# Logit products of a linear-attention, cosine-FFN and soft-MoE kernel gathered from four groups a block into two, with a longer ring of activation tiles

## The chip, the cores and the metric

The kernel runs on one core of one Trainium2 chip. The metric is device time in microseconds (us) of one execution. TensorE (PE) multiplies matrices into PSUM; VectorE (DVE) and ScalarE (ACT) do the elementwise work; GpSimd (POOL) does little here; SyncE (SP) issues the DMAs. Each engine takes its own instructions in program order, so an instruction that waits holds up all that stand behind it on that engine.

## What is computed

```python
# attention: 8 batches, 8 heads, 576 tokens, head size 64
kv  = einsum('bhsd,bhse->bhde', k, v)
out = einsum('bhsd,bhde->bhse', q, kv)
x   = out / sqrt(mean(out*out, -1) + 1e-6) * g_norm     # 4608 tokens x 512
# feed-forward: 512 -> 2048 -> 512
h = x @ w_in
g = h * cos(h)
x = g @ w_out
# soft mixture of experts: 8 experts x 4 slots = 32 slots
logits = x @ phi
d = softmax over tokens(logits);  slot_input = d.T @ x
slot_out[e] = relu(slot_input[e] @ w1[e]) @ w2[e]
return softmax over slots(logits) @ slot_out
```

## The kernel before

The 4608 tokens are cut into `NB` = 12 blocks j of `TB` = 384 tokens, and the 2048 columns of h into `NF` = 16 tiles f of 128. A step is one (j, f). The order of the work on every engine is written out by hand: at each step the program runs what is registered in `loads` (DMAs), then `main`, then `side` (other TensorE work and what goes with it), `cos_a`, `post`, `cos_b`, `cos_c`, `fin`. `at2(j, f, ...)` registers an entry in `side`; an f of 16 or more belongs to the next block, so "step 18 of block j" is step 2 of block j+1. Blocks 0 and 1 are interleaved; blocks 2 to 11 run one after the other. Block 11 and the expert layers behind it (`tail`) are ordered differently.

`main` (L378) computes one tile of h: twelve products of 128x128 by 128x384 into one of three PSUM banks of the pool `ps_m`. The cosine is a chain between ACT and DVE: `fr` (L396) and `tt` (L398) on ACT, the rounding (L403) on DVE, the sine (L408) on ACT, and the product g = h cos h (L443) on DVE, which is the last reader of the bank. So the product `main` of tile f+3 needs the L443 of tile f. The result lies in a slot of `ring`, 128x384 each. In blocks 2 to 10 DVE then transposes it into `tr` (L449), from where `regroup` DMAs bring it to `g`.

`w_out` and `phi` are folded into `wp`, so the logits of a block are 16 products of 128x32 by 128x384, one a tile, in `logits` (L491): four neighbours write the four quarters of the partitions of one bank. In blocks 2 to 10 there were four calls, `c` = 0 to 3, at steps 6, 10, 14 and 18 (`4 * c + PLAN["lg"]`), each taking four tiles out of the ring. `l_evac` (L510) copies the bank at step 18, `l_add` (L516) sums the quarters at step 19, then `l_max`, `l_exp`, `l_T` (L561, step 22) and `slot_acc` (L585, step 26, "ab") follow for the running softmax over tokens.

The attention of block j+1 is computed inside block j: `att_out` (L203) at steps 4, 8 and 11, `att_xs` (L224) one step later, `att_xT` (L235 on TensorE, then L239 on ACT) at steps 7, 11 and 14, `att_lo` (L248 on DVE). `kv_pair` (L184, L187) computes k'v for two heads, followed by two copies into `kvA` (L140, on DVE); four of them make a batch. For batches 4 to 7 they stand in blocks 4, 5, 7 and 8, two at step 14 and two at step 18. They, `att_out`, `att_xT`, `l_add`, `l_T` and `slot_acc` share the four PSUM banks `ps_a`.

`ring_next` hands out the first free slot of the ring: seven slots, and three more in blocks 0 and 1. `load_q` brings q for block j into one of two buffers, `q0` and `q1`, at step 13 of block j-2. Late in the kernel, `fill` loads the experts' weights, in a fixed order of pieces of 256 KB, into buffers that are free by then, `q0` at step 13 of block 9 and `q1` at step 12 of block 10 among them; `tail` refills them in the order of the lists `early` and `mid`.

Of the kernel before, what the change touches and what calls it, by code (L numbers as in the profile page):

```python
# [8 lines left out]
F32 = mybir.dt.float32  # L9
# [12 lines left out]
PLAN = dict(  # L22
    ke=(0, 0),
    lp=(0, 0, 0),
    wE=0,
    gE=(0, 0),
    nt=(1, (12, 16, 20, 24), (1, 2), (2, 1), (3, 1), 4),
    rx=0,
    nq=(0, 0),
    nl=3,  # L30
# [10 lines left out]
    stop=None,  # L41
    start=(
# [4 lines left out]
    ),  # L47
# [3 lines left out]
    pm=3,  # L51
    pa=4,
    lag=0,
    lg=6,
    le=18,
    la=19,
    lx=(3, 1),
# [6 lines left out]
    xs=(1, 1, 1),  # L64
    xT=(7, 11, 14),
    lo=(1, 0, 0),
    kv=(14, 14, 18, 18),
    rg=(11, 18),
    kvl=0,
    ql=13,  # L70
# [4 lines left out]
def tile_linear_attention__ffn_cos__soft_moe(  # L75
# [19 lines left out]
    NB = qT.shape[0]  # L95
    TB = qT.shape[2] * qT.shape[4]

    SP = 2
    const = ctx.enter_context(tc.tile_pool(name="const", bufs=1))
    w_p = ctx.enter_context(tc.tile_pool(name="w", bufs=1))  # L100
    x_p = ctx.enter_context(tc.tile_pool(name="x", bufs=1))
    g_p = ctx.enter_context(tc.tile_pool(name="g", bufs=1))
    t_p = ctx.enter_context(tc.tile_pool(name="t", bufs=1))
    gt_p = ctx.enter_context(tc.tile_pool(name="gt", bufs=1))
    dr_p = ctx.enter_context(tc.tile_pool(name="dr", bufs=1, space=bass.MemoryType.DRAM))
    tmp_p = ctx.enter_context(tc.tile_pool(name="tmp", bufs=2))
    kv_p = ctx.enter_context(tc.tile_pool(name="kvp", bufs=4))
    rem_p = ctx.enter_context(tc.tile_pool(name="rem", bufs=1))
    q_p = ctx.enter_context(tc.tile_pool(name="qp", bufs=1))
# [23 lines left out]
    ring = [[None, gT_all[:, i, :], 0] for i in range(7)]  # L133
# [16 lines left out]
        return [(0, 128, 2 * p + (i if i < 2 else t // 2))]  # L150

    def load_q(j):
        t = q_p.tile([128, 3, 4, 128], F32, tag=f"q{j % 2}", name="q")
        if j == 0:
            for t3 in range(3):
                nc.sync.dma_start(out=t[:, t3], in_=qT[j][:, t3])
        else:
            nc.sync.dma_start(out=t, in_=qT[j])
        q_t[j] = t
# [204 lines left out]
    h_t, gT_t, g_t, tr_t = {}, {}, {}, {}  # L364

    def on_pe(j, f):
        return j < 2 or j == NB - 1
# [63 lines left out]
        run(fin, j, f)  # L431

    def ring_next(j, f):
        i = next(i for i, r in enumerate(ring) if (r[0] not in gT_t or j == NB - 1)
                 and (not r[2] or j == 0 or j == 1 and f < 10))
        _, g, extra = ring.pop(i)
        ring.append([(j, f), g, extra])
        return g

    def cos_c(j, f):  # L440
        fr = fr_t.pop((j, f))
        g = ring_next(j, f)
        nc.vector.tensor_tensor(out=g, in0=fr, in1=h_t.pop((j, f)), op=ALU.mult)  # L443
        gT_t[j, f] = g
        if not on_pe(j, f):
            h, o = divmod(f, 8)
            if o == 0:
                tr_t[j, h] = t_p.tile([128, 12, 8, 32], F32, tag=("TA", "TB")[h], name="tr")
            nc.vector.transpose(out=tr_t[j, h][:, :, o, :], in_=g.rearrange("p (b t) -> p b t", t=32))  # L449
# [36 lines left out]
    def logits(j, c):  # L486
        if c == 0:
            l_t[j] = ps_l.tile([128, TB], F32, tag="l", name="l")
        for o in range(4):
            f = 4 * c + o  # L490
            nc.tensor.matmul(out=l_t[j][32 * o:32 * o + 32, :], lhsT=wp[:, f, :], rhs=gT_t.pop((j, f)),  # L491
                             start=(c == 0), stop=(c == (2 if j == NB - 1 else 3)))

    def logits2(j, f):
        if (j, f) == (0, 0):
# [329 lines left out]
    def at(j, f, fn, *a):  # L825
        side.setdefault((j, f), []).append((fn, a))
# [8 lines left out]
    def U(j, f):  # L835
        if j == 0 and f >= NF:
            j, f = 1, f - L
        return j + f // NF, f % NF

    def at2(j, f, *a):  # L840
        at(*U(j, f), *a)
# [6 lines left out]
    def end(j, f, fn, *a):  # L848
        fin.setdefault((j, f), []).append((fn, a))
# [6 lines left out]
    def ld_at(j, f, fn, *a):  # L856
        loads.setdefault(U(j, f), []).append((fn, a))

    for j in range(NB):
        for f in range(NF):  # L860
            if on_pe(j, f):
                at2(j, f + (1 if j == 1 and f < NF // 2 else 2), gtr, j, f)
        for h in range(2):
            if (j, h) == (NB - 2, 1):
                for x in range(4):
                    ld_at(NB - 1, x + PLAN["lag"], regroup, j, h, (x,))
            elif not on_pe(j, 8 * h):
                for x in range(4):
                    ld_at(j, PLAN["rg"][h] + x * PLAN["rx"], regroup, j, h, (x,))
        if j == 0:  # L870
            for f in range(NF):
                at2(0, f + PLAN["wT"], wp_kk, f)
                at2(0, f + PLAN["wM"], wp_sum, f)
        if j < 2:
            for f in range(0, NF, 2):
                late_in = j and f + 3 + L >= NF - (L < 6)
                at2(*((1, f + 3) if late_in else (0, f + 3 + L * j)), logits2, j, f)
        if j < NB - 1:
            for c in range(4 * (j > 1)):
                at2(j, 4 * c + PLAN["lg"], logits, j, c)  # L880
            le, la, lx, how = PLAN["E"][j] if j < 2 else (PLAN["le"], PLAN["la"], *PLAN["lx"])
            at2(j, le, l_evac, j)
            at2(j, la, l_add, j)
            at2(j, la, l_max, j)
            (at2, late2, end2)[how](j, NF + lx, l_exp, j)
        else:
            for c in range(3):
                at2(j, 4 * c + 6, logits, j, c)
            at2(j, 14, l_evac, j)
            at2(j, 15, l_add, j)  # L890
            for f in range(12, NF):
                side.setdefault((j + (f + 2) // NF, (f + 2) % NF if f > 13 else 15), []).insert(0 if f > 13 else 99, (l_add, (j, f)))
            at2(j, 18, l_max, j)
            at2(j, 18, warm, 5)
            end(NB, 3, l_exp, j)
            at(NB, 0, exp_table)
# [8 lines left out]
    for b in range(1, B):  # L905
        p, i = divmod(b, 2)
        n, sl = 3 * p - 2 + i, PLAN["kv"]
        if b < 4:
            n, sl = PLAN["K"][b - 1]
# [3 lines left out]
    for j in range(1, NB):  # L913
        n = j - 1
# [8 lines left out]
    for j in range(2, NB):  # L923
        ld_at(j - 2, PLAN["ql"], load_q, j)
    for b in range(2, B):
        p, i = divmod(b, 2)
        n = 3 * p - 2 + i
# [18 lines left out]
    for u in range(2 * NF):  # L946
        n = (j0 + u // len(ns)) * NF + ns[u % len(ns)]
# [4 lines left out]
        ld_at(*divmod(n + nd, NF), nat_store, u)  # L952
    for n in range(4):
        ld_at(9, 12, fill, kv_p, "kv", 2)
    ld_at(9, 13, fill, q_p, "q0", 3)
    ld_at(9, 14, fill, const, "sp", SP)
    ld_at(10, 12, fill, q_p, "q1", 3)
    ld_at(10, 13, fill, const, "kvA", 2)
    ld_at(9, 11, fill, rem_p, "vr", 1)
    ld_at(9, 13, fill, const, "ex", 1)  # L960
# [7 lines left out]
    ld_at(11, 8, fill, g_p, "g0", 6)  # L968
    for n in range(8, 15):
        ld_at(11, n + 1, fill, w_p, f"w{n}", 2)  # L970
    early = [(kv_p, "kv", 2)] * 4 + [(q_p, "q0", 3), (const, "sp", SP), (q_p, "q1", 3),
             (const, "kvA", 2), (rem_p, "vr", 1), (const, "ex", 1), (rem_p, "kr", 2), (x_p, "x0", 6)]
    mid = [(t_p, "TB", 6), (g_p, "g0", 6)] + [(w_p, f"w{n}", 2) for n in range(8, 15)] + [(x_p, "x1", 6), (gt_p, "gt", 5)]
    Z = []

    def sel_init():
# [32 lines left out]
    def token(t, f):  # L1009
        k, *arg = t.split(".")  # L1010
        if k.upper() in steps:
            out = int(k.islower())
            w = int(arg[0]) if arg else f + (PLAN["LO"] if out else PLAN["LI"])
            if w < NF and (arg or w >= (PLAN["PO"] if out else PLAN["PI"])):
                ck(k.upper(), w, out)
                steps[k.upper()](w, out)
        elif arg:
            a = int(arg[0])
            dict(kv=lambda: kv_pair(0, a), ao=lambda: att_out(0, a), xs=lambda: att_xs(0, a),
                 xT=lambda: att_xT(0, a), lo=lambda: att_lo(0, a), warm=lambda: warm(a),  # L1020
                 win=lambda: load_win(a), wout=lambda: load_wout(a), lkv=lambda: load_kv(a // 4, a % 4),
                 rem=lambda: load_rem(a) if a == 0 else load_kz(0, 1), q=lambda: load_q(a))[k]()
        else:
            j = int(k[1])
            f -= L * j
            if 0 <= f < NF:
                dict(m=main, s=lambda j, f: run(side, j, f), f=fr_tt, r=round_off, p=lambda j, f: run(post, j, f),
                     b=cos_b, c=cos_c, e=lambda j, f: run(fin, j, f), l=lambda j, f: run(loads, j, f))[k[0]](j, f)
# [107 lines left out]
```

## Time and profile before

| | us |
|---|---|
| median of three runs | 700.54 |
| lowest and highest of them | 698.97 and 700.83 |
| the profiled execution | 698.78 |
| its span, first to last instruction | 696.3 |

The granted TensorE clock averaged 0.99 over the span. A profiled execution is one execution; busy times and starts below are of it, and 698.78 - 696.3 = 2.5 us lie around its span.

### The profile page before, as it was taken

To read this page: it belongs to the slowest core of one execution; us is meant where nothing else is said; L and a number is where in the kernel's file an instruction comes from. 1 tells how busy PE (TensorE), PEld (TensorE's weight loads), DVE (VectorE), ACT (ScalarE), POOL (GpSimd) and SP (SyncE) were. 2 spreads that over 40 slices of the span, in tenths; PEclk is the share of its full clock that TensorE was granted. 3 is DMA by queue.
4 is the path that set the end of the run, shared out by engine and by line. 5 is a ranking of instruction groups with operands and counts; after the bars stand their busy time and mean duration, and the time that the engine had idled before them with its cause. 6 is when DMAs were issued, how large, how long until landed. Compare 5 with 4: busy or idle time off the path is not lost.

```text
span 696.3 us, 13667 instructions
## 1 busy us (share of the span) xinstructions
PE 666.7 (96%) x5109; PEld 558.0 (80%) x5109; DVE 523.6 (75%) x1092; ACT 442.5 (64%) x944; POOL 107.1 (15%) x104
## 2 busy tenths in 40 slices
PE   7769999999999999999999999999999999999994
PEld 6659998886888888888897879888979797874363
DVE  3998998477888878888888888888887875444144
ACT  3778997675676676676576765766757657662143
POOL 2351334100402111112012021110120210000500
PEclk9999999999999999999999999999999999999996
DMA  8963552022742574763634846826338469999998
GB/s 325 389 224 128 181 186 87 17 89 92 216 115 72 135 224 137 208 184 87 171 76 109 241 135 187 216 75 170 83 91 305 104 163 294 327 373 350 394 380 363
DMA packets 68144, 134.12 MB, mean 193 GB/s; under 512 B 8432, under 2 KB 40304, under 8 KB 67312
## 3 DMA queue, kind: packets, MB, share of 16 engines
q1 hardware_dynamic: 68080, 133.27, 60.1%
q8 instruction: 40, 0.66, 0.4%
q14 instruction: 24, 0.20, 0.1%
HBM read 91.29 MB, written 13.63 MB: 151 GB/s over the span
## 4 chain that ended last, share of the span: by engine, by line
PE 71%; DVE 11%; ACT 9%; DMA 3%; issue 2%; SPq 1%; POOL 0%; DVEq 0%
PE h L378 43%; PE ab L585 4%; PE l L491 4%; PE ops L203 3%; PE xTps L235 2%; PE tr L464 2%; PE eo L755 2%; DVE gT L443 2%; ACT fr L408 2%; PE eh L729 2%; DVE tt L403 2%; PE kvps L184 2%; DVE tr L449 2%; ACT L408 1%; ACT L540 1%
## 5 line engine op out<-in xcount | busy, mean ns | idle before, releaser
L378 PE MATMUL h<-xt,w 128*128 128x384 f32 (+1 forms) x2316 | 436.2, 341 | 3.3 <-DVE xt L248 1.6
L378 PEld LDWEIGHTS h<-xt,w 128*128 128x128 f32 x2316 | 397.4, 188 | 27.0 <-DVE gT L443 7.3
L408 ACT ACTIVATE fr<-tt 128x384 f32<-128x384 f32 x191 | 99.9, 524 | 134.1 <-DVE tt L403 133.7
L443 DVE TENSOR_TENSOR gT<-fr,h 128x384 f32<-128x384 f32 x185 | 102.2, 553 | 57.9 <-ACT fr L408 57.7
L215 POOL TENSOR_TENSOR ri<-ss,mhalf 128x8 f32<-128x8 f32 x36 | 66.1, 1839 | 415.2 <-DVE ss L213 415.2
L403 DVE SCALAR_TENSOR_TENSOR tt<-tt,fr 128x384 f32<-128x384 f32 x191 | 104.3, 550 | 21.5 <-ACT tt L398 20.5
L398 ACT ACTIVATE tt<-fr 128x384 f32<-128x384 f32 x191 | 100.3, 525 | 6.1
L396 ACT ACTIVATE fr<-h 128x384 f32<-128x384 f32 x191 | 91.7, 480 | 10.6 <-PE h L378 10.6
L449 DVE STREAM_TRANSPOSE tr<-gT 128x384 f32<-128x384 f32 x144 | 83.3, 579 | 5.0
L203 PE MATMUL ops<-kvA,q 128*128 128x128 f32 (+1 forms) x320 | 37.9, 277 | 1.8 <-ACT g L140 1.8
L203 PEld LDWEIGHTS ops<-kvA,q 128*128 128x128 f32 (+1 forms) x320 | 35.0, 180 | 4.1 <-ACT g L140 2.1
L239 ACT ACTIVATE xt<-xTps,gn 128x512 fp32r<-128x512 f32 x36 | 24.5, 683 | 21.6 <-PE xTps L235 21.6
L315 POOL TENSOR_TENSOR w<-st_m,w 128x512 fp32r<-128x512 f32 x16 | 26.8, 1677 | 52.5 <-ACT w L310 43.4
L491 PE MATMUL l<-gT,wp 128*32 128x384 f32 x312 | 33.3, 498 | 0.0
L248 DVE SCALAR_TENSOR_TENSOR xt<-xTps,gn,xt 128x512 fp32r<-128x512 f32 x36 | 26.4, 739 | 8.4 <-ACT xt L239 8.1
L585 PE MATMUL ab<-g,d 128*32 128x512 f32 x264 | 30.4, 593 | 0.0
L140 ACT COPY g<-tr 128x384 f32<-128x384 f32 (+1 forms) x64 | 23.4, 392 | 8.7 <-PE tr L464 5.4
L184 PEld LDWEIGHTS kvps<-kv 128*64 128x64 f32 x512 | 17.6, 137 | 10.0 <-issue 7.0
L212 DVE TENSOR_REDUCE ss<-sq 128x8 f32<-128x512 f32 x33 | 22.1, 671 | 4.5 <-ACT sq L210 4.1
L224 DVE TENSOR_TENSOR xs<-ops,ri 128x512 f32<-128x512 f32 x33 | 22.3, 681 | 2.4 <-PE tr L464 1.5
L210 ACT ACTIVATE sq<-ops 128x512 f32<-128x512 f32 x33 | 19.5, 589 | 6.6 <-PE ops L203 6.6
L184 PE MATMUL kvps<-kv 128*64 128x64 f32 x512 | 20.6, 226 | 2.0 <-DMA kv<-in_kv 2.0
(146 smaller groups left out, 629.4 us busy)
## 6 DMA issues: line engine op xcount, KB each, us to landing
g<-tr SPq DMA_DIRECT2D x288, 96.0 KB
kv<-in_kv SPq DMA_DIRECT2D x32, 512.0 KB
ew<-in_w SPq DMA_DIRECT2D x19, 512.0 KB
out<-ot SPq DMA_DIRECT2D x12, 768.0 KB
q<-in_qT SPq DMA_DIRECT2D x11, 768.0 KB
rw<-in_w_in SPq DMA_DIRECT2D x16, 512.0 KB
st_b<-in_w_outT SPq DMA_DIRECT2D x16, 512.0 KB
ew<-in_w SPq DMA_DIRECT2D x6, 1024.0 KB
```

The costliest lines, as they stand in the source:

```text
L184: nc.tensor.matmul(out=ps[h], lhsT=t[:, 0, r, h], rhs=t[:, 1, r, h], start=(r == 0), stop=False)
L203: nc.tensor.matmul(out=ps[p0:p0 + n, pr * 128:(pr + 1) * 128], lhsT=q_t[j][:, t, pr, p0:p0 + n], rhs=kvbd[b % 2][:, pr, :], start=True, st ...
L215: nc.gpsimd.tensor_tensor(out=ri[:, :, 0], in0=ss, in1=mhalf, op=ALU.pow)
L378: nc.tensor.matmul(out=ps, lhsT=w[:, a, kk, :], rhs=x[:, b, kk, s], start=(n == 0), stop=(n == 3 * KD - 1))
L396: nc.scalar.activation(out=fr, in_=ps, func=AF.Copy, bias=0.25, scale=INV_2PI)
L398: nc.scalar.activation(out=tt, in_=fr, func=AF.Copy, bias=ROUND_M)
L403: nc.vector.scalar_tensor_tensor(out=tt, in0=tt, scalar=-ROUND_M, in1=fr, op0=ALU.add, op1=ALU.subtract)
L408: nc.scalar.activation(out=fr, in_=tt, func=AF.Sin, scale=-TWO_PI_DOWN)
L443: nc.vector.tensor_tensor(out=g, in0=fr, in1=h_t.pop((j, f)), op=ALU.mult)
L449: nc.vector.transpose(out=tr_t[j, h][:, :, o, :], in_=g.rearrange("p (b t) -> p b t", t=32))
L491: nc.tensor.matmul(out=l_t[j][32 * o:32 * o + 32, :], lhsT=wp[:, f, :], rhs=gT_t.pop((j, f)), start=(c == 0), stop=(c == (2 if j == NB - 1 ...
L585: nc.tensor.matmul(out=ps[32 * c:32 * c + 32, :], lhsT=d[:, t, :], rhs=gs[c // 2][t][:, (c % 2) * 512:(c % 2) * 512 + 512], start=(t == 0) ...
```

## The change

The logits of blocks 2 to 10 are issued in two groups of eight tiles, at steps 10 and 18, in place of four groups of four at steps 6, 10, 14 and 18. Tiles therefore stay longer in the ring, which gets four more slots from step (2, 0) on until step (11, 1). They lie in the place of the second query buffer: `q1` holds only block 1's q, and all others use `q0`. All four `kv_pair` of a batch stand at step 18, behind the second group of logits. In block 11 the ring no longer hands out slots that are still in use. The expert weights that went to `q0` and `q1` are loaded later: `q0` at step 12 of block 10, `q1` at step 7 of block 11, and `q1` moves from `early` to `mid`.

```diff
-    lg=6,
+    lg=10,
-    kv=(14, 14, 18, 18),
+    kv=(18, 18, 18, 18),
...
     def load_q(j):
-        t = q_p.tile([128, 3, 4, 128], F32, tag=f"q{j % 2}", name="q")
+        t = q_p.tile([128, 3, 4, 128], F32, tag="q1" if j == 1 else "q0", name="q")
...
     def ring_next(j, f):
-        i = next(i for i, r in enumerate(ring) if (r[0] not in gT_t or j == NB - 1)
-                 and (not r[2] or j == 0 or j == 1 and f < 10))
+        if (j, f) == (2, 0):
+            more = q_p.tile([128, 4, TB], F32, tag="q1", name="gT")
+            ring.extend([None, more[:, i, :], 2] for i in range(4))
+        i = next(i for i, r in enumerate(ring) if r[0] not in gT_t
+                 and (not r[2] or r[2] == 1 and (j == 0 or j == 1 and f < 10) or r[2] == 2 and (j, f) < (NB - 1, 2)))
...
     def logits(j, c):
-        for o in range(4):
-            f = 4 * c + o
+        n = 4 if j == NB - 1 else 8
+        for i in range(n):
+            f, o = n * c + i, i % 4
             nc.tensor.matmul(out=l_t[j][32 * o:32 * o + 32, :], lhsT=wp[:, f, :], rhs=gT_t.pop((j, f)),
-                             start=(c == 0), stop=(c == (2 if j == NB - 1 else 3)))
+                             start=(f < 4), stop=(f >= (8 if j == NB - 1 else 12)))
...
-            for c in range(4 * (j > 1)):
-                at2(j, 4 * c + PLAN["lg"], logits, j, c)
+            for c in range(2 * (j > 1)):
+                at2(j, 8 * c + PLAN["lg"], logits, j, c)
...
-    ld_at(9, 13, fill, q_p, "q0", 3)
+    ld_at(10, 12, fill, q_p, "q0", 3)
...
-    ld_at(10, 12, fill, q_p, "q1", 3)
+    ld_at(11, 7, fill, q_p, "q1", 3)
```

## Rows read from the trace of the kernel before

**Rows 1.** The page, engines: busy us, share of the span, instructions.
```profile
PE 666.7 (96%) x5109; PEld 558.0 (80%) x5109; DVE 523.6 (75%) x1092; ACT 442.5 (64%) x944; POOL 107.1 (15%) x104
```

**Rows 2.** Waits from 210 to 575 us: us in total, times, longest.
```profile
PE h L378 <- DVE gT L443: 1.3, 3, 0.4
...
ACT xt L239 <- PE xTps L235: 14.8, 16, 1.5
```

**Rows 3.** Timeline of PE, block 7, steps 6 to 10: start, us, instructions, idle before.
```profile
398.85 2.38 PE L378 MATMUL h<-xt,w 128*128 128x384 f32 x12 [0.42 <-DVE gT L443]
401.16 0.85 PE L491 MATMUL l<-gT,wp 128*32 128x384 f32 x8
...
402.28 2.35 PE L378 MATMUL h<-xt,w 128*128 128x384 f32 x12
404.47 0.60 PE L235 MATMUL xTps<-ident,xs 128*128 128x128 f32 x4
404.82 2.34 PE L378 MATMUL h<-xt,w 128*128 128x384 f32 x12
...
412.50 0.85 PE L491 MATMUL l<-gT,wp 128*32 128x384 f32 x8
413.16 2.76 PE L585 MATMUL ab<-g,d 128*32 128x512 f32 x24
```

**Rows 4.** Timeline of DVE: the products that free the banks; the kvA copies.
```profile
398.24 0.55 DVE L443 TENSOR_TENSOR gT<-fr,h 128x384 f32<-128x384 f32 x1 [0.92 <-ACT fr L408]
...
401.23 0.56 DVE L443 TENSOR_TENSOR gT<-fr,h 128x384 f32<-128x384 f32 x1 [0.59 <-ACT fr L408]
...
433.54 0.55 DVE L443 TENSOR_TENSOR gT<-fr,h 128x384 f32<-128x384 f32 x1 [0.26 <-ACT fr L408]
...
439.47 0.93 DVE L140 COPY kvA<-kvps 64x64 f32<-64x64 f32 x4
```

**Rows 5.** Timeline of ACT: L239 of step 14 or 11; L396 of (8, 3).
```profile
381.32 0.69 ACT L239 ACTIVATE xt<-xTps,gn 128x512 fp32r<-128x512 f32 x1 [0.20 <-PE xTps L235]
...
418.70 0.69 ACT L239 ACTIVATE xt<-xTps,gn 128x512 fp32r<-128x512 f32 x1 [0.91 <-PE xTps L235]
...
428.53 0.69 ACT L239 ACTIVATE xt<-xTps,gn 128x512 fp32r<-128x512 f32 x1 [1.51 <-PE xTps L235]
...
441.45 0.47 ACT L396 ACTIVATE fr<-h 128x384 f32<-128x384 f32 x1
```

**Rows 6.** Timeline of PE, from step 14 of block 7 to (8, 3).
```profile
425.74 0.85 PE L491 MATMUL l<-gT,wp 128*32 128x384 f32 x8
426.52 0.69 PE L184 MATMUL kvps<-kv 128*64 128x64 f32 x16
...
427.15 0.64 PE L184 MATMUL kvps<-kv 128*64 128x64 f32 x16
...
427.83 0.66 PE L235 MATMUL xTps<-ident,xs 128*128 128x128 f32 x4
428.25 8.58 PE L378 MATMUL h<-xt,w 128*128 128x384 f32 x48
436.75 0.85 PE L491 MATMUL l<-gT,wp 128*32 128x384 f32 x8
...
438.85 2.37 PE L378 MATMUL h<-xt,w 128*128 128x384 f32 x12
```

**Rows 7.** Timeline of ACT, block 9, step 14.
```profile
522.86 0.69 ACT L239 ACTIVATE xt<-xTps,gn 128x512 fp32r<-128x512 f32 x1 [0.54 <-PE xTps L235]
```

**Rows 8.** Stretches at the end: busy us per engine, PEclk, DMA share, GB/s.
```profile
608.00:612.00 4.00, 4.00 (x27) 3.93 (x26) 1.71 (x4) 2.69 (x7) 0.00 (x0) 1.00 0.87 282
...
624.00:632.00 8.00, 6.94 (x127) 3.95 (x131) 2.46 (x9) 1.68 (x7) 0.00 (x0) 1.00 0.81 289
632.00:676.00 44.00, 43.69 (x435) 21.37 (x425) 16.35 (x25) 11.52 (x22) 9.78 (x36) 1.00 1.03 393
676.00:684.00 8.00, 6.38 (x40) 5.05 (x39) 5.35 (x9) 4.84 (x11) 0.00 (x0) 1.00 0.82 335
```

More of the change, by code (lines that the diff above doesn't have):

```diff
@@ L970, in tile_linear_attention__ffn_cos__soft_moe @@
         ld_at(11, n + 1, fill, w_p, f"w{n}", 2)
-    early = [(kv_p, "kv", 2)] * 4 + [(q_p, "q0", 3), (const, "sp", SP), (q_p, "q1", 3),
-             (const, "kvA", 2), (rem_p, "vr", 1), (const, "ex", 1), (rem_p, "kr", 2), (x_p, "x0", 6)]
-    mid = [(t_p, "TB", 6), (g_p, "g0", 6)] + [(w_p, f"w{n}", 2) for n in range(8, 15)] + [(x_p, "x1", 6), (gt_p, "gt", 5)]
+    early = [(kv_p, "kv", 2)] * 4 + [(q_p, "q0", 3), (const, "sp", SP), (const, "kvA", 2), (rem_p, "vr", 1), (const, "ex", 1), (rem_p, "kr", 2), (x_p, "x0", 6)]
+    mid = [(q_p, "q1", 3), (t_p, "TB", 6), (g_p, "g0", 6)] + [(w_p, f"w{n}", 2) for n in range(8, 15)] + [(x_p, "x1", 6), (gt_p, "gt", 5)]
     Z = []
```

## The prediction, made before the changed kernel ran

> **What bounds the kernel now.** I read the busy times first, then the waits of the long middle (210 to 575 us), then the timelines of PE, DVE and ACT through two kinds of block, and last the DMA load of the end. PE is busy 96% of the span [rows 1], so the change looks as if each us taken off PE were a us won. The waits say otherwise. In 365 us PE idles only 1.3 us in three longer waits, all before `main` and for the product L443 that frees a bank; ACT waits for PE 14.8 us in sixteen waits, all for the transposes of the attention [rows 2]. So two chains run side by side, PE and ACT/DVE, and each stops for the other at a fixed place in every block. What the reader is to see is where.
>
> In block 7, `main` 6 waits 0.42 us and starts at 398.85 [rows 3], 0.06 after the L443 of tile 3 has ended (398.24 + 0.55 = 398.79 [rows 4]). From there PE runs without a stop to the transposes of step 11. There ACT, which is early, waits 0.91 us for them [rows 5]. At step 14 ACT waits again: 0.20 us where the step holds logits and transposes (block 6), 1.51 us where two `kv_pair` stand there too (block 7) [rows 5], 0.54 us in block 9, where ACT has less to do [rows 7]. From step 14 to the next block's step 6, ACT/DVE set the pace and PE comes to `main` 6 early. One turn is thus: PE from step 6 to step 11, ACT/DVE from there to step 14, a wait there, ACT/DVE to the next step 6. I work out the shift of each of these points against before.
>
> The pages of the Trainium skill bear on this: "Perfetto Trace Analysis", section "Optimization Strategy", says that a gap that repeats on the engine that should be full can mean too few buffers for the next tile. By that rule more room in the ring would not help here, since the room that lacks is in PSUM. The trace agrees with its 0.42 us before `main`.
>
> **What each group of logits costs PE.** Step 6 with logits and the small L561 takes 402.28 - 398.85 = 3.43 us; step 7 with four transposes takes 404.82 - 402.28 = 2.54 [rows 3]. The difference, 0.89, is a lone group. A second group straight behind a first is not in the trace; the nearest row is the group followed by the likewise narrow L585, 413.16 - 412.50 = 0.66 [rows 3]. Bounds: 0.5 (narrow products overlap better yet) to 0.89 (nothing is shared). I take 0.66. Per block PE then sheds 2 x 0.89 at steps 6 and 14 and takes on 2 x 0.66 at 10 and 18: 0.46 us, in nine blocks 4.1 us of PE's work.
>
> **Step 6 to step 11.** With the logits gone PE would be at `main` 7 0.89 us earlier. But `main` 7 needs the L443 of tile 4, which ends at 401.23 + 0.56 = 401.79 [rows 4], only 0.49 before `main` 7 starts now [rows 3]; PE resumes 0.06 after a release, so it gains 0.43 and idles 0.46. Tile 4's product depends on nothing of PE that is late, so this bank stays where it is. Later banks do not stop PE: `main` 8 starts at 404.82, and the next product falls well ahead of it. At step 10 the doubled group adds 0.66. Step 11 is reached 0.66 - 0.43 = 0.23 us **later** in each block, and ACT, which already waits there 0.91 us, takes on all of it.
>
> **Step 14.** Now logits are gone from here too, and PE is early. In a block without `kv_pair` ACT gives back the 0.20 us it waited: the turn comes out at 0.23 - 0.20 = +0.03 us. This holds for two turns (blocks 3 and 6). PE, ahead now, stops instead before `main` 1 and 2 of the next block.
>
> **The four `kv_pair`.** In blocks 4, 5, 7 and 8 step 14 loses two pairs as well (427.83 - 426.52 = 1.31 us [rows 6]). ACT gets its transposes 2.2 us earlier and gives back the whole 1.51: it runs at 0.23 - 1.51 = -1.28 us. At step 18 two things eat this. First DVE: four copies more, 0.93 us by the row of the four that are there now [rows 4], in front of a rounding that ACT waits for; before, such copies at step 14 lay in the shadow of ACT's wait. That alone leaves -0.35. Second PE: `main` 2 of block 8 starts three fourths into the 8.5 us of four mains, at about 434.6 [rows 6], 0.5 after its bank's release at 433.54 + 0.55 [rows 4], so it can move to -1.28 - 0.45 = -1.73 and no further. Then come 0.66 for four more logits and two more pairs at 427.15 - 426.52 = 0.63 each [rows 6], in all 1.92: `main` 3 starts at +0.19. ACT reads it now 0.23 after its end (441.45 against 438.85 + 2.37 [rows 5, 6]), so ACT can at best be at about 0.0 there, not at -0.35. At `main` 6 the turn comes out between 0.0 (ACT) and +0.19 (PE with no slack left); I take +0.05, as PE still waits a little there before. Four turns: +0.2.
>
> **The other turns.** Block 9 gives back 0.54 at step 14, so 0.23 - 0.54 = -0.31. Block 10 has the same wait, but behind it, in block 11, ACT copies PE's transposes of g, which stand behind the group at step 18 that is now 0.66 longer: I take 0, bounds -0.3 to +0.35. Entering the cycle, block 2 has other work at its steps and PE is not stopped at (3, 6); there PE's shed work shortens the way once, by at most the 0.46 of one block; I take -0.4, bounds -0.5 and 0.
>
> Sum: 2 x 0.03 + 4 x 0.05 - 0.31 + 0 - 0.4 = -0.45, taken as -0.5 us. With the lone group's 0.89 as the second group's price, each of the eight turns is 0.23 dearer (+1.8); with 0.5, 0.16 cheaper (-1.3).
>
> **What lies beside other work.** The ring: before, seven slots held up to six tiles when the next was asked for; now eleven hold up to ten. One stays spare in both, and a slot's reader is at the earliest the group of the same block's step 10, so DVE waits for no slot. `load_q` into the one `q0` must wait for `att_out` at step 11; it is issued behind the sixteen `regroup` DMAs of that step, which wait for "ab" at step 10, so this costs nothing, and q is needed five steps later. If that cover were gone, some us of SP's queue would follow, with `regroup` behind it, which has eight steps until "ab". The first `load_kv` of blocks 5 and 8 now wait on SP until step 2 of their block, about two steps; behind them stand a raw-weight load and `regroup`, each needed several steps on. The four pairs take all four banks of `ps_a`; `l_add`, one `main` later, needs the first of them, which DVE copied first: nothing.
>
> **The end.** Three pieces of weights (0.79 MB) fewer are there by block 10, and come in block 11. At 393 GB/s [rows 8] that is 2.0 us of DMA in a stretch that is full from 632 to 676 us. Before it DMA is idle 0.13 x 4 + 0.19 x 8 = 2.0 us, at 608 to 612 and 624 to 632, and behind it 0.18 x 8 = 1.4 us, up to 684 [rows 8]; the new load stands in the queue ahead of all these. I take 0; the other bound is +2.0.
>
> **Rivals.** *PE decides* (0.18): the stops at `main` 7, 1 and 2 do not bite, and 4.1 us come back: 696.4. For it speaks the 96%, against it the 0.49 us of room. The Trainium skill, "TensorEngine Tiling (Array Packing)", section "Key Properties", says that a change of the tiling mode drains TensorE. By that rule eighteen such changes fewer are a gain of their own, and the time would be this rival's; the trace agrees as far as 0.89 against 0.66 goes.
>
> *The burst at step 18* (0.13): something other than PE's transposes holds ACT at step 14 of the four blocks with pairs, so the 1.28 us do not come back, while 1.92 us still go to step 18. Then `main` 3 is at -0.45 + 1.92 = +1.5 and four turns cost 1.4 each: +5.6, about 706. It decides from 0.5 us a turn on. Against it: no other wait stands before that L239 now.
>
> *The weights come late* (0.09): the idle DMA time is not usable, +2.0 on -0.5: 702.0, still within the bound below.
>
> **How the numbers follow.** The likeliest, 0.60, is that the chains cancel: -0.5 us. The profiled execution would go from 698.78 to 698.3; it is the lowest of what is shown, and against the median of 700.54 I say 700.0. Its own range, with the second group's bounds, is 698.7 to 701.8. A measurement here tells about 0.3% (2.1 us) from no change. Faster: the first rival and the cheap end of the likeliest, 0.21. Slower: the burst and the upper corner of the weights with the dear second group, 0.15. Within: 0.64. The range reaches to the first rival and part of the way to the second: 696.4 to 703.5.
>
> **What would show it.** In the changed kernel: sixteen-instruction groups of logits of about 1.5 us; a stop of 0.4 to 0.5 us before `main` 7 of each block; PE's busy time down by some 4 us and its waits for L443 up by as much; ACT's wait at step 11 still 0.9 to 1.1, and no wait at step 14; eight copies in a row at step 2 of blocks 5, 6, 8 and 9. It is wrong if the stop before `main` 7 is missing, or if ACT still waits at step 14.

## The result, and the profile after

| | before | after |
|---|---|---|
| median of seven runs | 699.43 us | 702.84 us |
| lowest and highest | 697.70, 700.83 | 701.53, 704.60 |
| the profiled execution | 698.78 | 702.13 |
| its span | 696.3 | 700.4 |

The ratio of the times is 1.0051, 95% interval 1.0035 to 1.0067: slower by 2.4 to 4.7 us. The forecast was -0.5 us; 702.84 lies within its range, but the sign was given only 0.15.

The stops at `main` 7 and at step 11 are where the prediction put them. The waits of the long middle in the changed kernel, 210 to 575 us (us in total, times, longest), answer to [rows 2]:

```profile
ACT xt L239 <- PE xTps L235: 7.6, 8, 0.9
...
PEld h L378 <- DVE xt L248: 3.0, 8, 0.4
...
PE h L378 <- DVE gT L446: 2.1, 7, 0.3
...
ACT fr L396 <- PE h L378: 1.2, 4, 0.3
```

Sixteen waits of ACT for the transposes have become eight, all at step 11: the wait at step 14 is gone. PE stops seven times, once a block before `main` 7. The last line is new: four times ACT waits for `main` 3, in the blocks behind `kv_pair`. The line of PEld, PE's weight loads, is new as well: the stops that the prediction put before `main` 1 and 2 are not there; instead PE waits eight times for DVE's last attention tile (L248), inside `main` 0 of the next block. PE's waits for L446 (L443 before) rose from 1.3 to 2.1 us, not by some 4, and its busy time did not fall. The page of the changed kernel, to lay beside 666.7 in [rows 1]:

```profile
PE 667.2 (95%) x5109; PEld 561.7 (80%) x5109; DVE 522.8 (75%) x1092; ACT 442.4 (63%) x944; POOL 107.3 (15%) x104
```

The logits did become cheaper, by 3.8 us, about what was forecast. `ab` and `main` (436.2 us before, 438.5 after) took that up again; `main` 0, with its new wait, is some 0.34 us longer in each of eight blocks. The lines of the logits and of `ab`, first of before, then of after (busy us, mean ns, idle before):

```profile
L491 PE MATMUL l<-gT,wp 128*32 128x384 f32 x312 | 33.3, 498 | 0.0
L585 PE MATMUL ab<-g,d 128*32 128x512 f32 x264 | 30.4, 593 | 0.0
```

```profile
L589 PE MATMUL ab<-g,d 128*32 128x512 f32 x264 | 33.3, 593 | 0.0
L495 PE MATMUL l<-gT,wp 128*32 128x384 f32 x312 | 29.5, 492 | 0.0
```

The timeline of PE in block 7 after, steps 5 to 11, to lay beside [rows 3] (start, us, instructions, idle before):

```profile
397.84 3.85 PE L378 MATMUL h<-xt,w 128*128 128x384 f32 x19
401.62 0.40 PE L565 MATMUL ldT<-ident,ld 64*128 64x64 f32 x3
402.30 2.36 PE L378 MATMUL h<-xt,w 128*128 128x384 f32 x12 [0.29 <-DVE gT L446]
404.50 0.60 PE L235 MATMUL xTps<-ident,xs 128*128 128x128 f32 x4
404.85 2.34 PE L378 MATMUL h<-xt,w 128*128 128x384 f32 x12
...
408.14 4.45 PE L378 MATMUL h<-xt,w 128*128 128x384 f32 x24
412.52 1.50 PE L495 MATMUL l<-gT,wp 128*32 128x384 f32 x16
413.83 3.12 PE L589 MATMUL ab<-g,d 128*32 128x512 f32 x24
416.89 2.35 PE L378 MATMUL h<-xt,w 128*128 128x384 f32 x12
```

The stop before `main` 7 is there (0.29), and so is the sixteen-instruction group (1.50). But `ab` (L589) now takes 3.12 us where it took 2.76 [rows 3], for the same 24 instructions on the same shapes. From the first logits to `main` 11 it is 416.89 - 412.52 = 4.37 us. From `main` 10 to `main` 11 it is 6.33 to 6.67 us in the eight blocks with `ab`; before it was 5.53 in each. So the second group costs 0.80 to 1.14 us, in the mean 1.01, not 0.66.

The ends of ACT's waits in block 7 and in (8, 3), on ACT's timeline after, to lay beside [rows 5]:

```profile
419.72 0.69 ACT L239 ACTIVATE xt<-xTps,gn 128x512 fp32r<-128x512 f32 x1 [0.94 <-PE xTps L235]
...
427.93 0.67 ACT L239 ACTIVATE xt<-xTps,gn 128x512 fp32r<-128x512 f32 x1
...
442.19 0.49 ACT L396 ACTIVATE fr<-h 128x384 f32<-128x384 f32 x1 [0.29 <-PE h L378]
```

To see where time comes and goes I counted the start of `main` in each trace from `main` (2, 0), and took the difference to before. Much of the spread between executions lies ahead of (2, 0), which starts between 139.9 and 143.6 us, and at the end; between, equal code repeats within 0.05 us (before and kernel 5; kernel n is the one of experiment n below). For all kernels of this study that are compared by it:

| main | after | ab_first | weights_moved | kv_alone | logits_alone | two_groups_kv14 |
|---|---|---|---|---|---|---|
| (3, 6) | +0.13 | +0.09 | 0.00 | 0.00 | +0.13 | +0.09 |
| (4, 6) | -0.17 | -0.35 | 0.00 | 0.00 | -0.18 | -0.34 |
| (5, 6) | +0.30 | -0.36 | 0.00 | -0.32 | +0.08 | -0.40 |
| (6, 6) | +0.66 | -0.38 | -0.02 | -0.68 | +0.46 | -0.48 |
| (7, 6) | +0.93 | -0.48 | -0.05 | -0.70 | +0.70 | -0.56 |
| (8, 6) | +1.23 | -0.49 | -0.04 | -1.03 | +1.05 | -0.65 |
| (9, 6) | +1.64 | -0.47 | -0.03 | -1.34 | +1.38 | -0.71 |
| (10, 6) | +1.80 | -0.68 | -0.05 | -1.37 | +1.51 | -0.92 |
| (11, 6) | +2.43 | -0.40 | -0.08 | -1.37 | +2.15 | -0.65 |
| (11, 14) | +2.45 | -0.41 | -0.08 | -1.39 | +2.17 | -0.65 |

The change has lost 2.45 us by step 14 of block 11, a little in each turn from block 4 on. The rest is lost at the end. The DMA load there, first of before (691.5 to 697 us), then of after (694 to 699.5 us), each in 40 equal parts of 0.1375 us, the digits in tenths of sixteen engines:

```profile
DMA  9979969799798979969798895000000000000000
```

```profile
DMA  9798998979999897999970101101011010000000
```

Before, the engines stop together at 691.5 + 25 x 0.1375 = 694.9. After, they stop at 694 + 21 x 0.1375 = 696.9, except for what reads as a 1 here and there: one engine of sixteen, which goes on to 698.5 or a little more. The last output waits for it. These are my two points to explain: 0.36 us a block around `ab`, and some 1.7 us at the end.

### The profile page after: what moved, and what is told of

The parts are those of the page before. It is cut to its first block, busy times and chain, and to the rows that moved or that the text cites. A ratio compares the mean times of both kernels' runs of the same rounds, so it can differ in the third digit from the quotient of the medians.

```text
span 700.4 us, 13687 instructions
## 1 busy us (share of the span) xinstructions
PE 667.2 (95%) x5109; PEld 561.7 (80%) x5109; DVE 522.8 (75%) x1092; ACT 442.4 (63%) x944; POOL 107.3 (15%) x104
## 4 chain that ended last, share of the span: by engine, by line
PE 64%; DVE 18%; ACT 13%; issue 2%; DMA 2%; SPq 0%; DVEq 0%
PE h L378 36%; PE ab L589 5%; DVE gT L446 4%; ACT fr L408 4%; DVE tr L452 3%; PE ops L203 3%; DVE tt L403 3%; PE l L495 3%; PE tr L467 2%; PE eo L759 2%; PE eh L733 2%; PE kvps L184 2%; ACT tt L398 2%; ACT L408 1%; ACT L544 1%
## 5 line engine op out<-in xcount | busy, mean ns | idle before, releaser
L378 PE MATMUL h<-xt,w 128*128 128x384 f32 (+1 forms) x2316 | 438.5, 341 | 4.9 <-DVE gT L446 2.4
L446 DVE TENSOR_TENSOR gT<-fr,h 128x384 f32<-128x384 f32 x185 | 102.3, 554 | 57.9 <-ACT fr L408 57.8
L396 ACT ACTIVATE fr<-h 128x384 f32<-128x384 f32 x191 | 91.9, 481 | 12.2 <-PE h L378 12.2
L589 PE MATMUL ab<-g,d 128*32 128x512 f32 x264 | 33.3, 593 | 0.0
L239 ACT ACTIVATE xt<-xTps,gn 128x512 fp32r<-128x512 f32 x36 | 24.3, 680 | 13.1 <-PE xTps L235 13.1
L248 DVE SCALAR_TENSOR_TENSOR xt<-xTps,gn,xt 128x512 fp32r<-128x512 f32 x36 | 26.1, 729 | 6.2 <-ACT xt L239 6.2
L495 PE MATMUL l<-gT,wp 128*32 128x384 f32 x312 | 29.5, 492 | 0.0
L589 PEld LDWEIGHTS ab<-g,d 128*32 128x32 f32 x264 | 11.1, 109 | 17.3 <-issue 14.1
```

The lines of the kernel that those rows point to most:

```text
L378: nc.tensor.matmul(out=ps, lhsT=w[:, a, kk, :], rhs=x[:, b, kk, s], start=(n == 0), stop=(n == 3 * KD - 1))
L396: nc.scalar.activation(out=fr, in_=ps, func=AF.Copy, bias=0.25, scale=INV_2PI)
L589: nc.tensor.matmul(out=ps[32 * c:32 * c + 32, :], lhsT=d[:, t, :], rhs=gs[c // 2][t][:, (c % 2) * 512:(c % 2) * 512 + 512], start=(t == 0) ...
```

## The experiments

**1. ab ahead of the logits (ab_first).** What stands in front of `ab` on PE's sequencer, the part of PE that takes instructions in order, can be seen when the instructions of its line are listed (duration in ns lowest/median/highest, first and last start). Block 7, first before, then after:

```profile
L585 PE MATMUL ab<-g,d x24: 592/592/593, 413.2 to 415.3; 128*32 128x512 f32 x24
L585 PEldq EVENT_SEMAPHORE  x15: 51/51/51, 410.7 to 412.3; - x15
```

```profile
L589 PE MATMUL ab<-g,d x24: 589/592/592, 413.8 to 416.4; 128*32 128x512 f32 x24
L589 PEldq EVENT_SEMAPHORE  x15: 51/51/51, 412.5 to 414.1; - x15
```

Fifteen waits on semaphores, for the `regroup` DMAs that `ab` reads, take some 1.6 us in both: (412.3 - 410.7)/14 = 0.11 us from one to the next. Before, they run while `main` 10 still has products in PE's queue, and are over 0.9 us ahead of `ab`. After, they begin with the first logits (412.5), and the last of them (414.1) comes after `ab` should have begun. The edit puts the first group behind `ab`:

```diff
-            for c in range(2 * (j > 1)):
-                at2(j, 8 * c + PLAN["lg"], logits, j, c)
+            if j > 1:
+                at2(j, 8 + PLAN["lg"], logits, j, 1)
...
+        if 1 < j < NB - 1:
+            at2(j, PLAN["lg"], logits, j, 0)
```

> The changed kernel with one order turned round: at step 10 of blocks 3 to 10 the products L585 (ab) are issued ahead of the group of eight logits, not behind it. Nothing else differs. In the changed kernel the way from main 10 to main 11 takes 6.54 us in block 7, 1.01 more than before, where 0.66 was forecast. Theory 'semaphores': fifteen waits for DMA landings stand in PE's instruction stream in front of ab, at about 0.106 us each; before, they passed while the products ahead of them were still queued for the array (410.7 to 412.3 us, during main 10), now they come out while the short logits products drain (412.5 to 414.1 us) and ab starts late. With ab straight behind main 10 they are covered again: main 10 to main 11 takes 5.53 + 0.65 = 6.2 us, block 11 is reached 8 x 0.35 = 2.7 us earlier than in the changed kernel, the time is about 700.1 (ratio to the kernel before near 1.001). Rival 'array': two narrow groups in a row cost the array itself more than 0.66; then the order makes no difference, main 10 to main 11 stays at 6.5 us, and the time at 702.8.

Measured: median 699.97 us, ratio 1.0015 [1.0001, 1.0028]. Block 7 on PE's timeline:

```profile
410.95 2.78 PE L589 MATMUL ab<-g,d 128*32 128x512 f32 x24
413.55 1.47 PE L495 MATMUL l<-gT,wp 128*32 128x384 f32 x16
414.95 1.34 PE L378 MATMUL h<-xt,w 128*128 128x384 f32 x6
```

The same 40 instructions take 414.95 - 410.95 = 4.00 us, against 4.37, and `main` 10 to `main` 11 is 6.18 = 5.53 + 0.65 us in all eight blocks. By step 14 of block 11 the loss of +2.45 has become -0.41.

**2. The moved weights alone (weights_moved).** Before, with the change's use of `q0` and `q1`:

```diff
-        t = q_p.tile([128, 3, 4, 128], F32, tag=f"q{j % 2}", name="q")
+        t = q_p.tile([128, 3, 4, 128], F32, tag="q1" if j == 1 else "q0", name="q")
...
-    ld_at(9, 13, fill, q_p, "q0", 3)
+    ld_at(10, 12, fill, q_p, "q0", 3)
...
-    ld_at(10, 12, fill, q_p, "q1", 3)
+    ld_at(11, 7, fill, q_p, "q1", 3)
```

and `q1` moved from `early` to `mid`.

> The kernel before with the query buffers and the weight loads of the changed kernel alone (q0 filled at step 12 of block 10, q1 at step 7 of block 11, q1 refilled in the later list); logits, ring and k'v as before. Behind block 11 the changed kernel loses 1.4 to 2 us more than its PE does: PE ends 2.0 us later, the last transfer 3.6 us later. Theory 'late weights': 0.79 MB more have to move at the end, which is full; the time is 1.4 to 2.0 us above the kernel before (ratio 1.002 to 1.003). Rival 'absorbed', as forecast: the idle DMA time at 608 to 632 and 676 to 684 us takes them, ratio 1.000, and the last 1.6 us in the changed kernel's trace are one DMA engine that falls behind the others in that execution.

Measured: median 698.65 us, ratio 0.9995 [0.9978, 1.0012], -0.08 at block 11. Neither the single query buffer nor the late 0.79 MB costs anything that shows.

**3. The four pairs alone (kv_alone).** Before, with one line changed:

```diff
-    kv=(14, 14, 18, 18),
+    kv=(18, 18, 18, 18),
```

> The kernel before with all four kv_pair of a batch at step 18 (PLAN kv=(18, 18, 18, 18)) and nothing else changed. By the turn worked out in the prediction: ACT's wait at step 14 gives back 1.31 us in blocks 4, 5, 7 and 8, the four copies at step 18 take 0.95 of it, so -0.36 us a turn, -1.4 us in all, ratio 0.998. Rival 'burst': the four pairs and eight copies at one step cost the chain more than they give back: a turn gets 0.3 us or more dearer, ratio 1.002 or above.

Measured: median 699.12 us, ratio 1.0001 [0.9981, 1.0020]. In the trace each of the four turns is 0.31 to 0.36 us shorter, -1.39 at block 11, and elsewhere nothing moves. The time does not show it: its execution has the late DMA engine of the end as well, here for 1.75 us.

**4. The logits alone (logits_alone).** The change with the pairs back at steps 14 and 18:

```diff
-    kv=(18, 18, 18, 18),
+    kv=(14, 14, 18, 18),
```

> The changed kernel with k'v as before (two kv_pair at step 14, two at step 18), so the two groups of eight logits, the longer ring and the moved weights without the k'v part. Step 10 still has ab behind the logits. By the turns: step 11 is reached 1.01 - 0.43 = 0.58 us later; light turns +0.58 - 0.20 = +0.4; turns with pairs at step 14: the transposes come 0.89 - 0.58 = 0.3 earlier, ACT follows, -0.2 to -0.3 a turn instead of the +0.4 to +0.5 of the changed kernel. Block 11 is reached about 2.7 us earlier than in the changed kernel; time about 700 (ratio 1.001 to 1.002 with whatever the weights cost at the end). Rival: if the k'v part is not what the kv turns pay for, block 11 is reached as in the changed kernel, 2.0 us later than before, ratio 1.005.

Measured: median 700.82 us, ratio 1.0033 [1.0017, 1.0050], +2.17 at block 11. This missed; 7 says why. Its outputs end with all DMA engines within some 0.2 us of each other.

**5. Twelve more instructions on PE (before_plus12).** The changed program has more waits on PE's sequencer: PE's instructions of every kind in the trace, weight loads and waits among them, are 10449 after, 10438 before, 10446 with the pairs alone, 10441 with the logits alone. The page counts one more transfer of kind "instruction" on q8 (transfers, MB, share), first before, then after:

```profile
q8 instruction: 40, 0.66, 0.4%
```

```profile
q8 instruction: 41, 0.67, 0.4%
```

Of after, 689 to 691.2 us, the outputs' queue and q8:

```profile
q1 hardware_dynamic: 156, 0.86, 97.2%
q8 instruction: 1, 0.02, 2.7%
```

So a piece of some 16 KB (0.67 MB by 41) goes between the outputs, at 690.0 to 690.9 us. While it goes, fifteen packets of data are under way at a time in place of sixteen. If it holds up one of the sixteen engines, then before with longer filler work on PE should show the same. The edit lengthens a warm-up of PE early in the kernel, by twelve instructions that no result uses:

```diff
-        "lkv.2 rem.0 lkv.1 lkv.0 lkv.3 q.0 lkv.4 win.0 win.1 win.2 wout.0 warm.12 lkv.6 wout.1 kv.1 kv.2 "
+        "lkv.2 rem.0 lkv.1 lkv.0 lkv.3 q.0 lkv.4 win.0 win.1 win.2 wout.0 warm.15 lkv.6 wout.1 kv.1 kv.2 "
```

> The kernel before with three more warm-up products at its start (warm.15 for warm.12; twelve instructions more on PE), where PE waits for the first k and v anyway. Observed so far: in the three kernels with all kv_pair at step 18 (PE records 10446 to 10449) a 16 KB transfer of the instruction queue q8 starts at 686.7 to 690.0 us, among the last output transfers, and one DMA engine ends its outputs 1.5 to 1.7 us behind the others; in the three with 10438 to 10441 records it starts at 698 us or later or not at all, and all engines end together. Theory 'instruction transfer': what counts is the length of PE's instruction stream; with 10450 records the transfer falls among the outputs here too: one engine 1.5 us late, ratio 1.002, and every block up to 11 as before. Rival 'k'v': the late engine belongs to the moved k'v products (their loads or their place); then nothing changes here, engines end together, ratio 1.000.

Measured: median 700.34 us, ratio 1.0013 [0.9995, 1.0031]; -0.05 at block 11. The queues at 687.5 to 689.5 us, and the DMA load from 692 to 697.5 us:

```profile
q1 hardware_dynamic: 143, 0.77, 95.5%
q8 instruction: 1, 0.02, 3.0%
```

```profile
DMA  9896999989899896999971101011010110000000
```

The transfer is there, and so is the one engine that goes on from 694.9 to 696.4 or more. The counts agree over all kernels here: those with up to 10441 instructions on PE show 40 transfers, those with 10446 to 10450 show 41, and the longest (kernel 9, 10736) shows 42. Kernels 8 and 9 have the transfer among their outputs too, and one engine 1.76 and 1.55 us late, here and below against the median of the sixteen engines' ends. In the trace the effect is shown; in the time of this kernel alone the interval still touches 1.

**6. Twelve fewer instructions, with ab first (ab_first_minus12).** As kernel 1, with `warm.9` for `warm.12`.

> The kernel ab_first (the changed kernel with ab ahead of the logits at step 10) with three warm-up products fewer at its start: 10437 records on PE. Theory 'instruction transfer': no q8 transfer among the outputs, engines end together, 1.4 us less than ab_first: ratio to the kernel before 0.9995 (its PE reaches block 11 0.4 us early). Rival 'k'v': as ab_first, ratio 1.0015, one engine 1.5 us late.

Measured: median 699.32 us, ratio 0.9992 [0.9974, 1.0011]. The page counts 40 transfers on q8 again, and none stands between the outputs. The ratio went from 1.0015 to 0.9992, though the intervals overlap. In its profile the last engine still ends 1.14 us late. Kernel 7, also without the transfer, ends with one engine some 0.85 us late. So an engine can be late for another reason too; which one is open.

**7. Both groups, ab first, pairs at 14 and 18 (two_groups_kv14).** As kernel 1, with `kv=(14, 14, 18, 18)`. This was to keep what each part had won.

> The changed kernel with ab ahead of the logits at step 10 and with two of the four kv_pair back at step 14. Step 10 then costs 0.65 more than before, not 1.01; by the turns of the prediction, in turns with pairs at step 14 the transposes come 0.89 - 0.22 = 0.67 earlier and ACT follows, and step 18 gets 0.65 in place of 1.9: -0.56 us a turn; light turns 0; entering the cycle -0.35, block 9 -0.33, given back at block 11. Block 11 is reached 2.5 us earlier than before; no instruction transfer among the outputs (10441 records): ratio 0.9965. Rival: what the order gains at step 10 and what k'v gives at step 14 overlap, since both end in ACT's wait; then it is no better than ab_first's -0.4: ratio 0.9995.

Measured: median 699.12 us, ratio 0.9982 [0.9966, 0.9998]: faster than both kernels, if by little. But at block 11 it is at -0.65, not -2.5. The waits of its middle:

```profile
ACT xt L239 <- PE xTps L235: 14.4, 12, 1.6
...
PE h L378 <- DVE gT L446: 2.1, 7, 0.3
ACT fr L396 <- PE h L378: 1.4, 4, 0.4
```

The last line says what I had left out. Take the turn of block 4, with the start of ACT's L396 against before, counted from `main` (2, 0): step 11 makes it later by 0.25 (from -0.34 to -0.09), step 14 gives back 0.78 (to -0.87), and at `main` 3 of block 5, behind the longer step 18, ACT waits for PE and loses 0.46 (to -0.41). Net: -0.07. I had reckoned that what step 14 gives back is kept. It is kept only up to the point where ACT meets `main` 3, and step 18 has grown by 4.92 - 4.27 = 0.65. The prediction knew this limit for four pairs at step 18 and I forgot it for two.

**8. ab two steps later (ab_step12).** As kernel 7, with `ab` away from the logits:

```diff
-        at2(j, sa, slot_acc, j)
+        at2(j, sa + 2 * (1 < j < NB - 2), slot_acc, j)
```

> The kernel two_groups_kv14 with ab of blocks 2 to 9 two steps later, at step 12 in place of 10, behind the transposes of step 11 that ACT waits 0.9 us for. Theory: step 11 is reached 2.7 us earlier, ACT's wait there goes (0.9 + 0.2 us), and the light turns become as cheap as PE's own work, -0.6 us each in place of 0: block 11 is reached about 4 us earlier than before; PE has 10446 records here, so the instruction transfer falls among the outputs and takes 1.4 of it back: ratio 0.996 to 0.9965. Rival: ab at step 12 holds back main 13 and 14 and with them the transposes of step 14, ACT waits there for what it no longer waits at 11: block 11 as in two_groups_kv14, ratio 0.9985 with the transfer.

Measured: median 722.19 us, ratio 1.0322 [1.0290, 1.0354]. A wide miss. `main` 10 to `main` 11 is 3.60 us now, as meant, but the loss comes from SP. Its queue over the whole span, in kernel 7 and then in this one (waiting line, releaser: us in total, times, longest):

```profile
SPq L482 <- PE ab L589: 39.2, 8, 5.1
```

```profile
SPq L482 <- PE ab L589: 99.6, 8, 13.4
```

`regroup` (L482) may overwrite `g` only when `ab` has read it. It stands at step 11, and a later `ab` holds SP there up to 13.4 us; the loads behind it on SP start late. Waits of ACT and of PE in the middle of this kernel, and one of ACT's on its timeline:

```profile
ACT st_m L346 <- DMA st_n<-in_w_out: 20.8, 6, 4.0
...
PE ops L203 <- DMA q<-in_qT: 5.2, 1, 5.2
```

```profile
248.70 0.52 ACT L408 ACTIVATE fr<-tt 128x384 f32<-128x384 f32 x1 [0.74 <-DVE tt L403]
252.69 0.44 ACT L346 ACTIVATE st_m<-st_n 128x256 f32<-128x256 f32 x1 [3.46 <-DMA st_n<-in_w_out]
```

ACT, which prepares a raw weight there, waits six times for a load of that kind, 20.8 us in all, and in block 10 PE waits for q. In kernel 7 neither line has a wait in the middle. By the starts of `main` this kernel is 25.0 us behind kernel 7 at step 14 of block 11, and 24.35 behind before. Of the 25.0, 17.4 are lost between `main` 3 and 7 of blocks 4 to 9, where ACT's six waits lie, 6.2 between the same steps of block 10, and 1.7 between `main` 7 and 13, where `ab` now stands alone. The prediction had named such a price for `load_q`: some us of SP's queue if the cover of "ab" at step 10 were gone.

**9. The waits a step earlier (waits_a_step_early).** Kernel 1 changes an order, and so could have won by something else than the waits. Here the order stays that of the change, and only the waits move: behind `main` 9, eight products of 32 columns by one element read a column of each piece of `g`, into the bank of `ab`, which `ab` overwrites.

```diff
+    ab_ps = {}
...
+    def ab_touch(j):
+        ps = ab_ps[j] = at_bank("ab")
+        for h in range(2):
+            for x in range(4):
+                nc.tensor.matmul(out=ps[0:32, 0:1], lhsT=wp[:, 0, :], rhs=g_t[j, h][3][:, 0, x, 0, 0:1], start=True, stop=True)
...
-        ps = at_bank("ab")
+        ps = ab_ps.pop(j) if j in ab_ps else at_bank("ab")
...
+        if 1 < j < NB - 1:
+            at2(j, sa - 1, ab_touch, j)
```

> The changed kernel, order of step 10 kept (logits ahead of ab); behind main 9 stand eight products of 32 columns by 1 that read one column of each piece of g into ab's bank (overwritten later, so the result is untouched). They take the waits for the regroup DMAs one step earlier, where main 9's queued products cover them. My theory (the fifteen semaphore waits in front of ab are uncovered where they stand behind the short logits): main 10 to main 11 falls from 6.54 to about 6.18 us in the blocks with ab, and the record shows no run of waits ahead of ab. Rival (the order of a narrow group and ab, or ab's own data, costs the 0.36 us): it stays at 6.5. Step 9 gets dearer by 0.3 to 0.9 us for a lone narrow group, so in time I expect no gain: 702 to 705 us either way.

Measured, one run: 707.17 us (before beside it 698.33). The instructions of the new line and of `ab`'s in block 7, and PE's timeline:

```profile
L584 PEldq EVENT_SEMAPHORE  x15: 51/51/51, 410.2 to 412.4; - x15
...
L597 PE MATMUL ab<-g,d x24: 592/592/593, 417.3 to 419.4; 128*32 128x512 f32 x24
```

```profile
410.73 2.37 PE L378 MATMUL h<-xt,w 128*128 128x384 f32 x12
413.04 0.67 PE L584 MATMUL ab<-g,wp 128*32 128x1 f32 x16
413.63 2.38 PE L378 MATMUL h<-xt,w 128*128 128x384 f32 x12
415.94 1.50 PE L495 MATMUL l<-gT,wp 128*32 128x384 f32 x16
417.26 2.76 PE L597 MATMUL ab<-g,d 128*32 128x512 f32 x24
419.95 0.45 PE L378 MATMUL h<-xt,w 128*128 128x384 f32 x1
```

The fifteen waits have moved to `main` 9, where they are covered, and `ab` takes 2.76 again. From the first logits to `main` 11 it is 419.95 - 415.94 = 4.01 us, as in kernel 1 and not 4.37: with the order unchanged, the waits alone account for the 0.36. `main` 10 to 11 was 6.31 us, not the 6.18 that I expected, since `main` 10 now stands behind a narrow product and is itself slower by some 0.1 at its head. The new products cost more than they win: `main` 9 to 10 is 413.63 - 410.73 = 2.90 us, against 2.21 for step 9 in the change.

## Why the prediction was wrong

**The step that failed** is "At step 10 the doubled group adds 0.66." The term was mis-sized: it measured 1.01, above the 0.89 that was to be its upper bound. Of this 0.65 is the group, as forecast, and 0.36 is the waits in front of `ab` that `main` 10 had covered and sixteen short logits do not. Eight such steps make 8 x 0.36 = 2.9 us; with the waits covered (kernel 1) the middle comes out 2.45 + 0.41 = 2.86 us better. Kernels 1 and 9 show this from two sides. The prediction asked what covers the edits that it costed at nothing; it did not ask what covered the instruction that the group was put ahead of.

**The sum itself held.** Turn by turn, from step 6 of a block to step 6 of the next, with the waits covered (kernel 1, by the table above):

| turn of block | forecast | measured, ab first | measured, after |
|---|---|---|---|
| 2 and 3 | -0.4 + 0.03 | +0.09 - 0.44 | +0.13 - 0.30 |
| 4, 5, 7, 8 (pairs) | +0.2 | -0.02 | +1.54 |
| 6 | +0.03 | -0.10 | +0.27 |
| 9 | -0.31 | -0.21 | +0.16 |
| 10 | 0 (-0.3 to +0.35) | +0.28 | +0.63 |
| to block 11 | -0.45 | -0.40 | +2.43 |

That the totals agree within 0.05 is in part luck: the pairs came out 0.22 cheaper than forecast and block 10 0.28 dearer, and the errors cancel.

**Step 6 to 11.** `main` 7 was to gain 0.43 and to idle 0.46. Counted from `main` 6 it moved from 3.43 to 402.30 - 399.31 = 2.99 us, a gain of 0.44, and idled 0.29. So the lone group that left step 6 was worth 3.43 - 2.70 = 0.73, not 0.89: the four transposes of step 7, which the prediction set against the small L561 of step 6, cost some 0.16 less than it. At step 14 the group was worth 0.79 where pairs stay there (kernel 7) and 0.93 where none ever stood. With 2 x 0.65 taken on, PE sheds 0.22 to 0.36 us a block, not 0.46. At step 6 the stop takes up the error, so it did not matter for the turn.

**Step 14 and the pairs.** ACT's wait there is gone, and four pairs at step 18 cost no more than forecast: ACT meets `main` 3 with a wait of 0.29 us, at the limit that the prediction named, and the four turns came to -0.02 us with the waits covered, against +0.2. Alone, the pairs gain 0.34 a turn (kernel 3): the 1.31 of two pairs at step 14 less 0.97 for DVE's four extra copies, against 0.93 in the prediction. Eight copies in a row are on DVE's timeline of the changed kernel:

```profile
438.85 1.91 DVE L140 COPY kvA<-kvps 64x64 f32<-64x64 f32 x8
```

**The end.** "I take 0" was about the weights, and kernel 2 says that this is right. What I did not see is the instruction transfer. In the profiled executions the DMA engines other than the late one end 0.03 us later after step 14 of block 11 than before; the late one adds 1.74. With +2.45 that is 4.2 us; the medians differ by 3.4 [2.4 to 4.7]. The two executions differ by 3.35: the change's started 0.5 us faster, and the other 0.4 lies behind the last transfer and around the span. That before with twelve more instructions shows the same transfer and the same late engine makes the cause fairly sure. For what it costs in time, kernel 5 alone decides little: 1.0013 [0.9995, 1.0031]. All kernels together say more. Take off each one's time against before (by its ratio) what it had lost or won at step 14 of block 11. With the transfer among the outputs there remain +1.1 us (after), +1.5 (kernels 1 and 3) and +1.0 (kernel 5); without it -0.3 (kernel 2), +0.1 (4), -0.2 (6, at -0.35 there) and -0.6 (7). Each of these is uncertain by 1 to 1.4 us, but all four with the transfer lie above all four without it, by some 1.5 us in the mean. Kernel 8, whose times spread over 6 us, leaves -1.8 and does not fit; kernel 9 ran once.

**The rivals.** *PE decides* fell: PE stopped before `main` 7 as forecast, and in `main` 0 in place of `main` 1 and 2. By its rule from the Trainium skill ("TensorEngine Tiling (Array Packing)", "Key Properties": a switch of the tiling mode drains TensorE) each switch fewer is a gain; the trace agrees as far as 0.73 to 0.93 for a lone group against 0.65 for one in a pair, and no more of it reached the end. *The burst at step 18* fell: no turn with pairs lost anything by the pairs. *The weights come late* fell in kernel 2. The time came out on the slow side for two reasons that none of the three named.

## What to carry to other kernels

An instruction that reads what many DMAs wrote can carry many waits on PE's sequencer, here fifteen; before something short is put in front of it, look what long work those waits have been hidden behind. A stall that is given back at one step is kept only to the next place where the other engine has no slack, so follow it to the end of the turn, for every variant. A change of the number of instructions can alter the end of a kernel whose last us are a full DMA queue, so compare two versions at a point in the middle as well as by their time.

## What the runs showed of the hardware

- A wait on a semaphore that had already come cost 0.11 us of PE's sequencer (15 of them from 410.7 to 412.3), with no work of PE's in it. Behind the products of `main` 10 (before and kernel 1) and of `main` 9 (kernel 9) none of it showed; behind sixteen short logits 0.36 us did.
- In the busy times such a loss does not stand as idle: the idle time before `ab` is 0.0 in both kernels, while its busy time rose from 30.4 to 33.3 us, 3.12 in place of 2.76 us in block 7.
- Instruction pieces share the DMA engines with the data: while one of some 16 KB went between the outputs (0.93 us in the changed kernel), fifteen data packets were under way at a time in place of sixteen. One engine of sixteen then ended 1.74 to 1.77 us late in four executions (after, the pairs alone, before with twelve more, kernel 8), 1.55 us in kernel 9 and 1.48 us in kernel 1. Without such a piece the engines ended within some 0.2 us in before and kernels 2 and 4, but the last one 0.85 and 1.14 us late in kernels 7 and 6.
